# Spare products on TensorE, tiny scalings on ScalarE and a new listed order in a block-sparse attention and channel-mix kernel

## Chip, cores and metric

One core of a Trainium2 chip runs the whole program. The metric is the device time of one execution in microseconds (us). The kernel before takes 536.89 us, the median of three runs (535.77 to 537.21).

## What is computed

The input is four batches of eight heads, 768 positions of 64 features. A position belongs to one of 24 blocks of 32. The first and the last block attend to everything and are seen by all; every other block sees itself, its two neighbours, the two end blocks and three sampled ones. What attention gives is the input x of a channel mix.

```python
scores = np.where(mask, scale * q @ k.T, -1e9)
attn = np.exp(scores - max); attn = attn / (attn.sum(-1) + 1e-09)
x = attn @ v                                     # heads side by side: (4, 768, 512)
xk = mu_k * x + (1.0 - mu_k) * x_prev            # x_prev: x one position earlier
xr = mu_r * x + (1.0 - mu_r) * x_prev
k = np.maximum(xk @ w_k, 0.0)                    # 512 -> 1024
v = k * k @ w_v                                  # 1024 -> 512
return 1.0 / (1.0 + np.exp(-(xr @ w_r))) * v
```

The weights arrive as 64-bit floats.

## The kernel before

The batches are handled in two pairs. **Attention** of a pair is twelve units: one for the two end blocks (the wide unit, m = -1 in the names), eleven for two inner blocks each. In a unit, TensorE multiplies queries and keys (`s`, for the wide unit `sw`), VectorE masks and takes maxima (`nm`), ScalarE takes exponentials with the sums (`p`, `L`), TensorE turns the result over (`t`, copied to `pt`) and multiplies it with the values (`o`). `finish` (line 594) adds 1e-09 to the sums, takes reciprocals (both in `recip`, on VectorE, tile `R`), divides (`x`), and TensorE turns `x` over (`tx`), from where ScalarE copies it to `xt`. The first three units of the first pair (`direct`) add their mask on TensorE; `first_soft` (line 496) then takes four maxima in one reduction (`most`, L500) and scales the 128x4 result by -1/8 (L502), both on VectorE.

The **channel mix** works on tiles of 128 positions of a pair. `split_x` (line 682) takes the difference of neighbouring positions (`d`, L702, on VectorE or GpSimd), adds mu times it to x (`f`, L705), and cuts the result into a high and a low part. `gate` (`r`), `hidden` (`h`) and `products` (`v`) then multiply three terms of high and low parts on TensorE; this is most of its work. `weight` (line 258) prepares each of ten pieces of 1 MB of the weights: ScalarE brings the upper words into range (`wf`, L270), VectorE shifts and puts bits together (L275, L279, L282) or GpSimd multiplies by a sign (L287), then the high part (`w`, L180 or L182) and the low part (`w`, L289) are written. All ten are needed before the first `v` bank is complete.

What runs where, and when, is not decided in this code: every step is added to a plan, the strings in `PICK` name an engine for each step of a kind, and `ORDER` lists all steps. Each engine gets its steps in that order and works them off one after another, waiting on each for what it needs. Transfers are issued by the Sync engine (SP) in the same list.

```python
def spin(times, first=False, last=False):
    one = nc.const_aps.tensor(1.0, (P, 512), BF16)
    for i in range(times):
        nc.tensor.matmul(idle.ap, one[:, 0:P], one, ...)
plan.add(PE, lambda: spin(WARM, first=True), writes=[(idle,)])      # WARM = 10
plan.add(PE, lambda: spin(1, last=True), writes=[(idle,)])
```

These products of ones give nothing that is used. Ten stand at the start and one later.

Of the kernel before, what the change touches and what calls it, by code (L numbers as in the profile page):

```python
# [159 lines left out]
def block_sparse_attention_channel_mix(ctx: ExitStack, tc: tile.TileContext, kt, kd, kw, qw, qn, vt, vn, vw, blocks, own_near, mu_k, mu_r, w_k, w_v, w_r, out):  # L160
# [280 lines left out]
    turns_done = [0]  # L441
# [55 lines left out]
    def first_soft(s, p, nm, L, gi):  # L497
# [548 lines left out]
```

## Time and profile before

| what | value |
|---|---|
| median of 3 runs | 536.89 us (535.77 to 537.21) |
| the profiled execution | 534.2 us, span 532.4 us |
| TensorE matmul busy | 506.9 us, 95% of the span |
| VectorE busy | 370.9 us, 70% |
| ScalarE busy | 295.1 us, 55% |
| GpSimd busy | 238.4 us, 45% |
| mean granted TensorE clock | 0.99 |
| data read from HBM | 80.07 MB |

The span is the time from the first to the last instruction of one execution; 1.8 us of that execution lie around it. Busy shares are averages over the span: in the slices of the page TensorE shows 5 to 8 tenths in the first seven of forty and 9 in all later ones but the last.

### The profile page before, as it was taken

The page shows a single profiled execution, that of the slowest core. Times are in us where ns is not written, and L with a number is a line of the kernel's source. Part 1 is how long each engine was busy: PE and PEld are TensorE (multiplying, and loading weights), DVE is VectorE, ACT ScalarE, POOL GpSimd, SP SyncE. Part 2 cuts the span into 40 slices and gives each one's busy share as a digit, 9 for nine tenths or more (in the row PEclk, how much of TensorE's full clock was granted, in tenths as well). Part 3 has the DMA queues.
Part 4 walks back from the last instruction along what each step waited for, and adds up shares of the span by engine and source line. Part 5 has one row for each costly group of instructions (what it writes and reads, how often), then busy time and mean ns, then how long its engine had stood idle before and what let it go on. Part 6 is the DMA issues. An engine that isn't in the chain of part 4 may idle for free.

```text
span 532.4 us, 17563 instructions
## 1 busy us (share of the span) xinstructions
PE 506.9 (95%) x6911; PEld 407.6 (77%) x6911; DVE 370.9 (70%) x890; ACT 295.1 (55%) x728; POOL 238.4 (45%) x289
## 2 busy tenths in 40 slices
PE   7885799999999999999999999999999999999997
PEld 2554578878878878787887887888888878888886
DVE  5778899997686676579686787776787464635312
ACT  3778698975764672664365567464664353313212
POOL 0571356731851811255073265262367536726530
PEclk9997899999999999999999999999999999999999
DMA  8989786533777887658667877777856603000102
GB/s 295 402 300 324 242 313 216 199 127 115 221 224 230 239 278 231 210 179 271 202 197 265 269 214 219 234 213 228 271 161 183 200 25 95 0 21 20 41 1 79
DMA packets 48165, 103.23 MB, mean 194 GB/s; under 512 B 6929, under 2 KB 23442, under 8 KB 48082
## 3 DMA queue, kind: packets, MB, share of 16 engines
q1 hardware_dynamic: 47794, 101.72, 59.8%
q8 instruction: 54, 0.88, 0.7%
q10 hardware_dynamic: 288, 0.39, 0.2%
q14 instruction: 29, 0.24, 0.1%
HBM read 80.07 MB, written 6.29 MB: 162 GB/s over the span
## 4 chain that ended last, share of the span: by engine, by line
PE 56%; DVE 9%; SPq 6%; DMA 6%; issue 5%; ACT 2%; POOL 2%; DVEq 0%; ACTq 0%; POOLq 0%
PE v L777 18%; PE o L554 5%; PE r_0p L731 4%; DMA VR<-vt 3%; PE s L524 3%; PE r_1p L731 3%; SPq L471 3%; PE h_0p L751 3%; PE h_1p L751 3%; PE h_3p L751 2%; DVE p L435 2%; SPq L414 2%; PE h_2p L751 2%; DMA p<-tb 2%; DMA VR<-vw 1%
## 5 line engine op out<-in xcount | busy, mean ns | idle before, releaser
L777 PE MATMUL v<-w,k 128*128 128x512 f32 (+1 forms) x600 | 143.1, 389 | 0.3 <-DVE w L289 0.3
L777 PEld LDWEIGHTS v<-w,k 128*128 128x128 f32 x600 | 107.5, 188 | 25.6 <-issue 1.6
L435 DVE CUSTOM_DVE_ANT_1 p<-s,near_mask 128x256 f32<-128x256 f32 x152 | 84.9, 627 | 31.0 <-PE s L524 20.4
L440 ACT ACTIVATE p<-p,nm 128x256 f32<-128x256 f32 x152 | 76.3, 503 | 36.4 <-DVE nm L435 31.3
L467 DVE STREAM_TRANSPOSE tb<-p 128x1024 f32<-128x1024 f32 x30 | 37.0, 1236 | 14.7 <-ACT p L440 8.7
L524 PE MATMUL s<-KR,q 64*32 64x256 f32 x1216 | 38.6, 380 | 1.2 <-ACT KR L180 1.2
L780 DVE SCALAR_TENSOR_TENSOR z<-v,z 128x512 f32<-128x512 f32 (+1 forms) x25 | 16.5, 665 | 30.5 <-PE v L777 23.7
L554 PEld LDWEIGHTS o<-VR,p 128*32 128x32 f32 x1920 | 27.9, 110 | 7.7 <-issue 4.9
L180 ACT COPY KR<-keys 128x256 f32 (+1 forms) x71 | 25.6, 426 | 13.6 <-PE s L524 13.4
L554 PE MATMUL o<-VR,p 128*32 128x64 f32 x1920 | 30.4, 220 | 2.7 <-DMA VR<-vt 2.7
L182 POOL COPY KR<-keys 128x256 f32 (+2 forms) x52 | 21.7, 460 | 21.5 <-DMA v_ring<-vw 13.9
L731 PE MATMUL r_1p<-w,xr 128*128 128x512 f32 x120 | 30.7, 401 | 0.0
L524 PEld LDWEIGHTS s<-KR,q 64*32 64x32 f32 x1216 | 20.8, 106 | 12.5 <-issue 3.6
L731 PE MATMUL r_0p<-w,xr 128*128 128x512 f32 x120 | 30.3, 400 | 0.0
L440 ACT ACTIVATION_READ_ACCUMULATOR p<-p,nm 128x1 f32 x152 | 28.7, 189 | 0.0
L741 POOL TENSOR_TENSOR h_1k<-h_1k 128x512 f32<-128x512 f32 x10 | 11.2, 1122 | 34.7 <-ACT k L740 34.7
L731 PEld LDWEIGHTS r_0p<-w,xr 128*128 128x128 f32 x120 | 22.0, 188 | 5.6 <-ACT k L740 0.6
L731 PEld LDWEIGHTS r_1p<-w,xr 128*128 128x128 f32 x120 | 21.9, 188 | 5.3 <-ACT h_3k L739 0.4
L705 DVE SCALAR_TENSOR_TENSOR xr_1f<-xr_1d,mk,xt 128x128 f32<-128x128 f32 x48 | 22.3, 485 | 4.9 <-POOL xr_1d L702 2.9
L751 PE MATMUL h_2p<-xk,w 128*128 128x256 f32 x192 | 25.7, 285 | 0.0
L710 POOL TENSOR_TENSOR xr<-xr_0f,xr 128x256 fp32r<-128x256 f32 x11 | 8.3, 751 | 38.8 <-DVE xr L182 25.1
L751 PE MATMUL h_3p<-xk,w 128*128 128x256 f32 x192 | 24.9, 283 | 0.0
(209 smaller groups left out, 1103.2 us busy)
## 6 DMA issues: line engine op xcount, KB each, us to landing
VR<-vn SPq DMA_DIRECT2D x42, 512.0 KB, 4.7
VR<-vt SPq DMA_DIRECT2D x130, 128.0 KB, 3.5
p<-tb SPq DMA_DIRECT2D x120, 128.0 KB, 3.3
KR<-kd SPq DMA_DIRECT2D x18, 512.0 KB, 4.9
out<-z SPq DMA_DIRECT2D x23, 256.0 KB, 3.6
q<-qn SPq DMA_DIRECT2D x22, 256.0 KB, 4.8
keys<-kw SPq DMA_DIRECT2D x14, 384.0 KB, 6.4
raw<-w_k SPq DMA_DIRECT2D x4, 1024.0 KB, 7.5
```

The costliest lines, as they stand in the source:

```text
L180: nc.scalar.copy(to, of)
L182: engine(on).tensor_copy(to, of)
L435: nc.vector.tensor_tensor_reduce(out=dealt(p.ap[:, cs]), in0=cut(view()), in1=by, scale=-SCALE, scalar=3e+38 if first is None else nm.ap[: ...
L440: plan.add(ACT, lambda: nc.scalar.activation(p.ap[:, cs], p.ap[:, cs], AF.Exp, bias=nm.ap[:, col:col + 1], scale=-1.0, accum_out=L.ap[:, h ...
L467: plan.add(DVE, lambda: nc.vector.transpose(out=turned.ap.rearrange('p (k y c) -> p k y c', k=QB, c=BLK), in_=p.ap.rearrange('p (y k c) -> ...
L524: nc.tensor.matmul(s.ap[ROWS[j], row, a * 256:(a + 1) * 256].rearrange('p (x g a) -> p g a x' if carried else 'p (x a g) -> p g a x', g=2, ...
L554: nc.tensor.matmul(o.ap[ROWS[j], h * D:(h + 1) * D], held[gi][1](i, g, j), VR[values[j % PAIR][g]].ap[:, j // PAIR, h * D:(h + 1) * D], st ...
L705: nc.vector.scalar_tensor_tensor(out=part(f.ap[:, i, :]), in0=part(d.ap), scalar=mk.ap[:, which, c:c + 1], in1=x.ap[:, two, c, 0:TT], op0= ...
L731: nc.tensor.matmul(pr.ap[:, 0:512], xr.ap[:, a, c, :], wr[c].ap[:, w, :], start=c == 0 and m == 0, stop=c == CC - 1 and m == 2)
L751: nc.tensor.matmul(ph.ap[:, ff * PAIR * TT:(ff + 1) * PAIR * TT], wk[f // 4 * CC + c].ap[:, w, f % 4 * P:(f % 4 + 1) * P], xk.ap[:, a, c, ...
L777: nc.tensor.matmul(pv.ap[:, 0:width], hid[f][2](a), wv[f].ap[:, w, cs], start=f == 0 and m == 0, stop=f == FC - 1 and m == 2)
L780: plan.add(DVE, lambda pv=pv, cs=cs: nc.vector.scalar_tensor_tensor(out=z.ap[:, cs], in0=pv.ap[:, 0:width], scalar=unit, in1=z.ap[:, cs], ...
```

## The change

Three sorts of edit and a new table.

- Eight groups of three spare products (`FILLS, FILL`) may stand anywhere in the order between the first ten and the last one. They write the same unused tile.
- The scaling of the four maxima in the direct units and the addition of 1e-09 to the sums become steps with an engine of their own, VectorE or ScalarE by two new strings in `PICK`; the reciprocal is now a step apart, on VectorE. Five of the six scalings and ten of the 24 additions are given to ScalarE.
- The difference in `split_x` may be replaced, where `PICK` says `A`, by mu times x on ScalarE; the mix then adds (1 - mu) times the earlier position, for which a tile `rest` is made once. Of 72 such choices, of two instructions each, 21 are `A`; GpSimd has 29 in place of 44 and VectorE 22 in place of 28.
- `PICK` and `ORDER` are replaced as a whole.

```diff
+        plan.add(DVE, lambda: nc.vector.tensor_scalar(out=rest.ap, in0=mk.ap, scalar1=-1.0, scalar2=1.0, op0=ALU.mult, op1=ALU.add), reads=[(mk, 0, 1)], writes=[(rest,)])
...
     plan.add(PE, lambda: spin(WARM, first=True), writes=[(idle,)])
+    for i in range(FILLS):
+        plan.add(PE, lambda: spin(FILL), writes=[(idle,)])
     plan.add(PE, lambda: spin(1, last=True), writes=[(idle,)])
...
-        plan.add(DVE, lambda: nc.vector.tensor_scalar(out=nm.ap, in0=nm.ap, scalar1=-SCALE, scalar2=None, op0=ALU.mult), reads=[(nm, 'max')], writes=[(nm, 'max')])
+        def scaled(k=most_done[0] - 1):
+            if chosen('most', k) == ACT:
+                nc.scalar.mul(nm.ap, nm.ap, -SCALE)
+            else:
+                nc.vector.tensor_scalar(out=nm.ap, in0=nm.ap, scalar1=-SCALE, scalar2=None, op0=ALU.mult)
+        plan.pick('most', most_done[0] - 1, scaled, reads=[(nm, 'max')], writes=[(nm, 'max')])
...
-        def recip():
-            nc.vector.tensor_scalar(out=R.ap, in0=L.ap, scalar1=1e-09, scalar2=None, op0=ALU.add)
-            nc.vector.reciprocal(R.ap, R.ap)
+        def summed(k=sums_done[0] - 1):
+            if chosen('sum', k) == ACT:
+                nc.scalar.activation(R.ap, L.ap, AF.Copy, bias=1e-09)
+            else:
+                nc.vector.tensor_scalar(out=R.ap, in0=L.ap, scalar1=1e-09, scalar2=None, op0=ALU.add)
...
                 def dif(c=c, d=d, k=k):
+                    if chosen('dif', k) == ACT:
+                        nc.scalar.activation(part(d.ap), x.ap[:, two, c, 1:1 + TT], AF.Copy, scale=mk.ap[:, which, c:c + 1])
+                        return
...
+FILLS, FILL = (8, 3)
...
-    "near": "PPAA",
+    "sum": "DDDDAADDDDADADDAADAAADDA",
+    "near": "PPPP",
+    "most": "AAADAA",
-    "hi": "PDDAPPAAAD",
-    "lo": "PPDDPDDDDD",
+    "hi": "DDDAAAAAAD",
+    "lo": "DDDPDDDDDD",
...
-    13, 5, 6, 8, 0, 2, 3, 14, 16, 11, 15, 36, 12, 35, 1, 37, 56, 19, 21, 20, 22, 24, 23, 25, 55, 39, 40, 41, 26, 42,
+    2, 13, 0, 119, 3, 15, 14, 24, 20, 22, 28, 27, 23, 45, 44, 21, 64, 65, 84, 25, 31, 85, 112, 16, 29, 114, 30, 33,
```

Three places show what the order becomes.

VectorE from the sums of unit 1 to its division, before. `R_1` are the sums of unit 1, `nm_2_0` and `nm_2_1` the maxima of unit 2, `pt` copies for unit 1, `w_864` a low part of a weight, `x_0` and `x_1` the divisions of units 0 and 1:

```order
L603 TENSOR_SCALAR R_1_859<-L_1_648 128x8
L604 RECIPROCAL R_1_859<-R_1_859 128x8
L613 TENSOR_TENSOR x_0_862<-o_0_766,R_0_579 128x512
L500 TENSOR_REDUCE nm_2_0_887<-s_2_0_866 128x4
L502 TENSOR_SCALAR nm_2_0_887<-nm_2_0_887 128x4
L182 COPY pt_1_1_1_940<-t_1_1_1_930 128x512
L182 COPY pt_1_1_0_948<-t_1_1_0_935 128x512
L500 TENSOR_REDUCE nm_2_1_950<-s_2_1_895 128x4
L182 COPY pt_1_0_0_958<-t_1_0_0_953 128x512
L502 TENSOR_SCALAR nm_2_1_950<-nm_2_1_950 128x4
L289 TENSOR_TENSOR w_864<-wf_650,w_864 128x2x512
L613 TENSOR_TENSOR x_1_1033<-o_1_964,R_1_859 128x512
```

The same stretch on VectorE in the change:

```order
L618 TENSOR_SCALAR R_1_848<-L_1_671 128x8
L504 TENSOR_REDUCE nm_2_0_861<-s_2_0_824 128x4
L182 COPY pt_1_1_0_864<-t_1_1_0_856 128x512
L182 COPY pt_1_1_1_901<-t_1_1_1_843 128x512
L628 TENSOR_TENSOR x_0_922<-o_0_772,R_0_548 128x512
L624 RECIPROCAL R_1_848<-R_1_848 128x8
L504 TENSOR_REDUCE nm_2_1_931<-s_2_1_903 128x4
L247 TENSOR_SCALAR rest<-mk 128x8
L293 TENSOR_TENSOR w_938<-wf_815,w_938 128x2x512
L628 TENSOR_TENSOR x_1_1024<-o_1_943,R_1_848 128x512
```

Both scalings of maxima are gone from VectorE, one `pt` copy went to ScalarE, `rest` came in, and the low part ahead of `x_1` is of another weight.

TensorE behind the wide unit's turned result (`tx_-1`) and ahead of the first products with values (`o_0`), before:

```order
L608 MATMUL tx_-1_685<-ident,x_-1_679 128x128 x4
L449 MATMUL t_0_1_0_705<-ident,p_0_1_562 128x128 x4
L449 MATMUL t_0_0_1_719<-ident,p_0_0_400 128x128 x4
L449 MATMUL t_0_1_1_748<-ident,p_0_1_562 128x128 x4
L449 MATMUL t_1_0_1_756<-ident,p_1_0_647 128x128 x4
```

The same place in the change:

```order
L622 MATMUL tx_-1_699<-ident,x_-1_667 128x128 x4
L253 LDWEIGHTS const-bfloat16-1.0
L253 MATMUL idle<-const-bfloat16-1.0 128x512
...
L453 MATMUL t_0_1_0_736<-ident,p_0_1_473 128x128 x4
L453 MATMUL t_0_0_1_757<-ident,p_0_0_519 128x128 x4
L453 MATMUL t_1_0_1_767<-ident,p_1_0_670 128x128 x4
```

Six spare products (two groups, each product with its weight load) now stand between `tx_-1` and the next turning. The other six groups stand in pairs after the first half of the wide scores (`sw_0`), between `o_1` and `tx_1`, and right behind `tx_1`.

VectorE behind the division of unit 1, before:

```order
L613 TENSOR_TENSOR x_1_1033<-o_1_964,R_1_859 128x512
L275 TENSOR_SCALAR wf_889<-wf_889 128x1024
L282 SCALAR_TENSOR_TENSOR wf_889<-raw_743,wf_889 128x1024
L702 TENSOR_TENSOR xr_0_0d_1087<-xt_0_571 128x128
L705 SCALAR_TENSOR_TENSOR xr_0_0f_1089<-xr_0_0d_1087,mk,xt_0_571 128x128
L702 TENSOR_TENSOR xr_0_0d_1121<-xt_0_571 128x128
L705 SCALAR_TENSOR_TENSOR xr_0_0f_1089<-xr_0_0d_1121,mk,xt_0_571 128x128
```

The same stretch in the change:

```order
L628 TENSOR_TENSOR x_1_1024<-o_1_943,R_1_848 128x512
L279 TENSOR_SCALAR wf_853<-wf_853 128x1024
L286 SCALAR_TENSOR_TENSOR wf_853<-raw_725,wf_853 128x1024
...
L182 COPY KR<-keys_108 128x256
...
L182 COPY KR<-keys_108 128x256
L182 ISA
L182 COPY KR<-keys_108 128x256
L724 SCALAR_TENSOR_TENSOR xr_0_0f_1085<-xt_0_86,rest,xr_0_0d_1054 128x128
L724 SCALAR_TENSOR_TENSOR xr_0_0f_1085<-xt_0_86,rest,xr_0_0d_1087 128x128
```

Three copies of sampled keys came to VectorE here, and the first two differences left it for ScalarE.

## Rows read from the trace of the kernel before

**Rows 1.** Busy time by stretch: start:end, length, then each engine's busy us (instructions), clock, DMA.

```profile
0.00:40.64 40.64, 32.53 (x455) 17.97 (x455) 29.05 (x75) 24.92 (x53) 18.45 (x29) 1.00 0.92 331
40.64:63.87 23.23, 16.24 (x360) 12.10 (x360) 20.30 (x24) 17.70 (x44) 5.79 (x3) 0.78 0.89 301
63.87:110.69 46.82, 43.16 (x751) 34.77 (x751) 46.05 (x91) 42.88 (x110) 25.74 (x21) 1.00 0.62 216
...
111.00:480.00 369.00, 365.66 (x5112) 301.92 (x5112) 258.18 (x673) 196.20 (x500) 168.23 (x215) 1.00 0.63 192
```

**Rows 2.** Timeline of TensorE at the two cuts: start, duration, instruction, wait before it.

```profile
38.41 1.61 PE L592 MATMUL o_-1_249<-v_ring,ptw 128*64 128x64 f32 x46 [0.73 <-DMA v_ring<-vw]
...
110.73 1.43 PE L777 MATMUL v<-w,k 128*128 128x512 f32 x5 [0.32 <-DVE w L289]
```

**Rows 3.** TensorE's waits from 106 us on: total us, times, longest.

```profile
PE o L554 <- DMA VR<-vt: 2.7, 4, 1.2
```

**Rows 4.** Timeline of all engines, 40 to 112 us: small VectorE operations, GpSimd beside them, `x_1`.

```profile
41.24 0.15 DVE L502 TENSOR_SCALAR nm<-nm 128x4 f32<-128x4 f32 x1
...
52.82 2.04 DVE L603 TENSOR_SCALAR R<-L 128x8 f32<-128x8 f32 x1 [1.35 <-ACT p L507]
...
56.02 2.35 POOL L289 TENSOR_TENSOR w<-wf,w 128x1024 fp32r<-128x1024 f32 x1
...
56.82 1.57 DVE L502 TENSOR_SCALAR nm<-nm 128x4 f32<-128x4 f32 x1
...
63.87 0.69 DVE L613 TENSOR_TENSOR x<-o,R 128x512 f32<-128x512 f32 x1 [1.22 <-PE o L554]
```

**Rows 5.** VectorE's groups of instructions, 40.64 to 63.87 us: count, busy us, mean ns, idle.

```profile
L275 DVE TENSOR_SCALAR wf<-wf 128x1024 int32<-128x1024 int32 x3 | 2.0, 683 | 0.0
...
L182 DVE COPY pt<-t 128x512 f32<-128x512 f32 x3 | 2.0, 682 | 0.0
```

**Rows 6.** VectorE's groups, 63.87 to 110.69 us; the key copies from the groups of 0 to 111 us.

```profile
L182 DVE CAST xk<-xk_0f 128x512 fp32r<-128x512 f32 x2 | 1.2, 616 | 0.1
...
L702 DVE TENSOR_TENSOR xr_0d<-xt 128x128 f32<-128x128 f32 x2 | 0.6, 284 | 0.0
...
L182 DVE CAST xr<-xr_0f 128x256 fp32r<-128x256 f32 x1 | 0.3, 295 | 0.0
...
L182 DVE COPY KR<-keys 128x256 f32 x3 | 1.1, 395 | 1.1 <-DMA raw<-w_r 1.1
```

**Rows 7.** Timeline of VectorE, 40 to 112 us: the sums of unit 3.

```profile
88.50 1.26 DVE L603 TENSOR_SCALAR R<-L 128x8 f32<-128x8 f32 x1
```

**Rows 8.** Chain of waits up to 112 us: start, us, two masked maxima back to back.

```profile
83.45 1.01 DVE p L435 x2
```

**Rows 9.** Timeline of TensorE, 30 to 112 us, around the places of the spare products.

```profile
35.81 0.59 PE L479 MATMUL s<-first_mask,ident 128*128 128x512 bf16 x2 [0.66 <-ACT p L507]
...
49.40 3.42 PE L554 MATMUL o<-VR,pt 128*32 128x64 f32 x118 [1.81 <-DMA VR<-vn]
...
60.65 3.15 PE L554 MATMUL o<-early,pt 128*32 128x64 f32 x128
64.71 0.63 PE L608 MATMUL tx<-ident,x 128*128 128x128 f32 x4 [0.92 <-DVE x L613]
...
66.95 1.10 PE L524 MATMUL s<-KR,q 64*32 64x256 f32 x32 [1.17 <-ACT KR L180]
```

**Rows 10.** The page's costliest groups: count, busy us, mean ns of one, idle before.

```profile
L777 PE MATMUL v<-w,k 128*128 128x512 f32 (+1 forms) x600 | 143.1, 389 | 0.3 <-DVE w L289 0.3
```

**Rows 11.** Chain of waits of the whole span: value products of a later unit.

```profile
258.42 1.92 PE o L554 x128
```

**Rows 12.** Busy time by stretch (columns as in the first group), short stretches with a low clock.

```profile
46.00:48.00 2.00, 1.59 (x16) 1.02 (x14) 1.97 (x3) 0.00 (x0) 0.00 (x0) 0.51 1.02 387
...
60.00:62.00 2.00, 2.00 (x56) 1.67 (x58) 1.96 (x4) 2.00 (x6) 0.00 (x0) 0.50 1.00 362
```

**Rows 13.** ScalarE's groups of the whole span: the smallest plain conversion.

```profile
L180 ACT CAST xr<-xr_0f 128x256 fp32r<-128x256 f32 x9 | 3.6, 404 | 12.9 <-DVE xr_0f L705 12.9
```

More of the change, by code (lines that the diff above doesn't have):

```diff
@@ L199, in block_sparse_attention_channel_mix @@
     mk = fixed([P, 2, CC], F32, 'mk')
+    rest = fixed([P, 2, CC], F32, 'rest')
     early = [buf([P, 2, PAIR, DM], F32, f'w{5 * CC // 2 - 1 - i}', 1, f'early{i}') for i in range(EARLY_V // 2)]
@@ L440, in exp @@
         plan.add(ACT, lambda: nc.scalar.activation(p.ap[:, cs], p.ap[:, cs], AF.Exp, bias=nm.ap[:, col:col + 1], scale=-1.0, accum_out=L.ap[:, h:h + 1]), reads=[(p, *keys), (nm, col)], writes=[(p, *keys), (L, h)])
-    turns_done = [0]
+    turns_done, most_done, sums_done = ([0], [0], [0])
     def turn(parts, name):
@@ L501, in first_soft @@
         plan.add(DVE, most, reads=[(s,)], writes=[(nm, 'max')])
-        plan.add(DVE, lambda: nc.vector.tensor_scalar(out=nm.ap, in0=nm.ap, scalar1=-SCALE, scalar2=None, op0=ALU.mult), reads=[(nm, 'max')], writes=[(nm, 'max')])
+        most_done[0] += 1
+        def scaled(k=most_done[0] - 1):
[4 more added lines that the diff above has]
+        plan.pick('most', most_done[0] - 1, scaled, reads=[(nm, 'max')], writes=[(nm, 'max')])
         for i in range(4):
@@ L600, in finish @@
             tp = buf([P, CC, P], F32, 't', T_BUFS, f'tx{b}_{m}', ps)
[L602 to L604 removed]
+        sums_done[0] += 1
+        def summed(k=sums_done[0] - 1):
[3 more added lines that the diff above has]
+                nc.vector.tensor_scalar(out=R.ap, in0=L.ap, scalar1=1e-09, scalar2=None, op0=ALU.add)
         def tr():
@@ L608, in tr @@
                 nc.tensor.transpose(tp.ap[:, c, :], x.ap[:, c * P:(c + 1) * P], ident.ap)
-        plan.add(DVE, recip, reads=[(L, *range(H))], writes=[(R,)])
+        plan.pick('sum', sums_done[0] - 1, summed, reads=[(L, *range(H))], writes=[(R,)])
+        plan.add(DVE, lambda: nc.vector.reciprocal(R.ap, R.ap), reads=[(R,)], writes=[(R,)])
         def divide():
@@ L701, in dif, with mix @@
                 def dif(c=c, d=d, k=k):
+                    if chosen('dif', k) == ACT:
+                        nc.scalar.activation(part(d.ap), x.ap[:, two, c, 1:1 + TT], AF.Copy, scale=mk.ap[:, which, c:c + 1])
+                        return
                     engine(chosen('dif', k)).tensor_tensor(out=part(d.ap), in0=x.ap[:, two, c, 1:1 + TT], in1=x.ap[:, two, c, 0:TT], op=ALU.subtract)
-                def mix(d=d, c=c, i=i, f=f):
+                def mix(d=d, c=c, i=i, f=f, k=k):
+                    if chosen('dif', k) == ACT:
+                        nc.vector.scalar_tensor_tensor(out=part(f.ap[:, i, :]), in0=x.ap[:, two, c, 0:TT], scalar=rest.ap[:, which, c:c + 1], in1=part(d.ap), op0=ALU.mult, op1=ALU.add)
+                        return
                     nc.vector.scalar_tensor_tensor(out=part(f.ap[:, i, :]), in0=part(d.ap), scalar=mk.ap[:, which, c:c + 1], in1=x.ap[:, two, c, 0:TT], op0=ALU.mult, op1=ALU.add)
-                plan.pick('dif', k, dif, reads=[(x, *known)], writes=[(d,)])
-                plan.add(DVE, mix, reads=[(d,), (x, *known), (mk, which)], writes=[(f, i)])
+                plan.pick('dif', k, dif, reads=[(x, *known), (mk, which)], writes=[(d,)])
+                plan.add(DVE, mix, reads=[(d,), (x, *known), (mk, which), (rest,)], writes=[(f, i)])
             cs = slice(h * MIX, (h + 1) * MIX)
@@ L881 @@
 PICK = {
-    "turn": "DADAAAADADAAAAAADADDAAAAAAAADAAAAAADADAAAADADDDDDDDD",
-    "near": "PPAA",
-    "keys": "AAPDAPAPAAAAAAAADAPAPAADAAPPPPPDDAAPDAPAPADAAPAA",
+    "turn": "AAAADDAAAAADAAAAAADDAAAAAADDAAAAAADADDAAAAADDAADDDDA",
+    "sum": "DDDDAADDDDADADDAADAAADDA",
+    "near": "PPPP",
+    "keys": "AAPPPDPADAPAAAAADADDADADAAPAAPDDAPAPAPPPPPAAAAAA",
+    "most": "AAADAA",
     "mag": "AAAAAAAAAA",
     "sign": "PPDDPDPPDD",
-    "hi": "PDDAPPAAAD",
-    "lo": "PPDDPDDDDD",
-    "dif": "DPPPPPDPPPPDPPDPPDPPDDPDDPDDPDDPDPPDPDPDDPPPPDPDPPPPPDPPPDPDPPDPPDDDPDPP",
-    "mix": "DADDAAADADDDDDDAADDAADDADDAAADDDADDDDADADDDDDADDADDDDDDDDDADADDADDADDDDA",
-    "low": "DDDDDDPDDPPDDPPPDPDDDPPDDDDPDPPPDPDPPPPDDDDPPDPPDDDPPDDPPPDPPDPPDDDDDDPD",
+    "hi": "DDDAAAAAAD",
+    "lo": "DDDPDDDDDD",
+    "dif": "APPPPADAAPPDAPDDPDPAPPDPPADPDAPADPPDAPPAPPDPAPADDADADPDPDDDAAAPPPDADADAP",
+    "mix": "DAADADADADDDDADDDDDADDADDADDDADDDDDDDAAADDDDADDDDADDADAADADDAAADADAADDAD",
+    "low": "DDDDDDPDDPPDPPDDDDPDDDPPPPPDDPPPDDPPDPPPPDPPPPDDDPDDPDPDPPDDPPDDDDDPDDDP",
 }
 ORDER = [
[103 rows of a table removed]
[105 rows of a table added]
 ]
```

206 rows, old and new, of the table ORDER are left out of this document.

## The prediction

> **What bounds the kernel now.** I began with the busy time by stretch, cutting the run where VectorE divides the wide unit (40.64 us), where it divides unit 1 (63.87), and where it writes the last low part of a weight (110.69) [rows 1]. In the order PE, weight loads, VectorE, ScalarE, GpSimd the reader should see this: from 111 to 480 us TensorE is busy 365.66 of 369 us, so nothing but TensorE counts there; from 63.87 to 110.69 VectorE is busy 46.05 of 46.82, so VectorE sets when that stretch ends; from 40.64 to 63.87 VectorE has 20.30 of 23.23 and the DMA engines 0.89; before 40.64 the DMA engines have 0.92 and no engine is full. Next the timeline of TensorE at the cuts: the first ends when the last piece of the ring of values has landed (`o_-1`, 0.73 us of waiting for DMA), the last when the last low part is there (`v` waits 0.32 for VectorE) [rows 2]. Last the waits of TensorE behind 106 us: the largest is four waits for values, 2.7 us together [rows 3]. So a change is worth what it does to the moment of that last low part, plus any wait that it opens in the packed stretch. TensorE's useful work behind that moment is the same in both kernels.
>
> **Up to 40.64 us: 0.** VectorE takes on a conversion of a weight, one shift (both about 0.68, as L275 [rows 5]) and two low parts (at most 2.35 each, what GpSimd needs for one [rows 4]): under 6.1 us. It idles 40.64 - 29.05 = 11.6 us here [rows 1], and that cover goes only if all this lands behind the last value piece, which comes by the same transfers as before.
>
> **40.64 to 63.87 us: -3.1.** The scalings of maxima leave VectorE. By itself one takes 0.15 us; one that begins while GpSimd is in a 2.35 us product takes 1.57, and an addition to sums, as small, 2.04 [rows 4]. Three scalings stood here: -1.57 - 0.15 - 0.15. One `pt` copy goes to ScalarE (-0.68) and one shift went ahead of 40.64 (-0.68) [rows 5]. `rest` comes in, 128x8 like the sums; I take it clean, +0.15. Sum -3.1. The low end is -4.3: then the 1.22 us that `x_1` waits for `o_1` goes too [rows 4]. The high end is -1.2: `rest` stalls as the sums did, 2.04. I take the clean value because GpSimd has one low part left in this stretch and lost three conversions; the scalings on ScalarE go where it has 23.23 - 17.70 = 5.5 us idle [rows 1]. Late next, once VectorE is quicker, is `o_1`.
>
> That stall is where a rule of the Trainium skill speaks against the change: "Advanced Engine Details and Errata", section "VectorE Performance Modes", says that VectorE's second SBUF port is shared with GpSimd, and that the two block each other. The trace agrees (1.57 beside GpSimd, 0.15 without). By that rule any small addition left on VectorE can still stall, whoever took the scalings; its time is in the second rival.
>
> **63.87 to 110.69 us: +0.6.** VectorE is full here, so each operation counts. In: three copies of keys, +1.1; one conversion of `xr`, +0.3; one more `pt` copy, +0.7; two masked maxima, +1.0 [rows 5, 6, 8]. Out: one conversion of `xk`, -0.6; two differences, -0.6 [rows 6]; the addition to the sums of unit 3, -1.26 [rows 7]. Sum +0.6. Low end -0.4, if the two maxima merely took the place of other work; high end +1.9, if the 1.26 stall passes to another small operation. The two differences cost ScalarE at most 0.40 each, its smallest conversion of twice as many elements [rows 13]; it idles 3.9 us here.
>
> **Spare products: +0.5.** Two products of this shape take 0.59 us [rows 9], and one of 512 columns lasts 0.389 by itself [rows 10], so each further one adds about 0.20 and a pair of groups, six products, takes between 1.2 (in line) and 1.4 (by itself); I take 1.3. The pair behind `sw_0` lies beside waits of 0.66 and 0.73 [rows 2, 9]. The pair behind `tx_-1` lies ahead of `o_0`, which waits 1.81 for values anyway [rows 9]. The pair before `tx_1` lies in its 0.92 us of waiting for the division: +0.4; the pair behind it in the 1.17 that the next scores wait for keys: +0.1 [rows 9]. At half clock each product takes 0.4 and the two pairs cost +2.7; below nothing they can only go through the clock.
>
> **Clock: -0.6.** The granted clock is 0.51 around 47 us and 0.50 around 61 us, the 1.2 GHz level, each time behind stretches in which TensorE waited [rows 12]. `o_0` takes 3.42 and `o_1` 3.15 there [rows 9], the same products 1.92 at full clock [rows 11]. `o_1` is on VectorE's path, since `x_1` waits for it. At full clock -1.2, unchanged 0; I take half, because the spare products stand at some of the waits ahead of it.
>
> **Behind 111 us: 0.** ScalarE takes on 42 scalings of `x` and 15 tiny ones, under 0.40 each [rows 13]: 23 us at most, against 369 - 196 = 173 idle in the packed stretch alone [rows 1]. GpSimd loses work. Best case -2.7, all four waits for values gone [rows 3]; worst case in the third rival.
>
> **Sum:** -3.1 - 0.6 + 0.6 + 0.5 = -2.6 us. The profiled execution took 534.2 and would take 531.6; the median, 2.7 above it, goes from 536.89 to **534.3 us**. With the ends of single terms this case lies between 531 and 536.
>
> **Rivals.**
> 1. *The spare products hold the clock.* Then `o_0` takes 1.92 (-1.5) and `o_1` gains 1.2 where I took 0.6: 534.3 - 1.5 - 0.6 = 532.2 us. For it: two of the pairs lie in the very gaps behind which the clock was low. Against it: two pairs stand behind `o_1`, too late for it, and `o_0` waits 1.81 for its values, so a faster `o_0` needs an earlier transfer only in part. The Trainium skill, "TensorE: Matmul & The Clock Gate", section "HAM oscillation — how this bites in real kernels", says that a wait between bursts of matmuls drops the clock, so that the next burst starts cold. The trace agrees with the drop (0.51 behind the waits); that spare work prevents it, no run here shows.
> 2. *No change.* Up to 64 us the DMA engines are 0.92 and 0.89 busy [rows 1]. The same bytes pass, in another order; if `o_0` and the weights go on waiting for them, VectorE's saving becomes idle time: 536.9. Or the stalls stay: `rest` at 2.04 and the two left-over additions give -2.6 + 1.9 = -0.7, so 536.2. For it: `o_-1` and `o_0` stand waiting for transfers [rows 2, 9]. Against it: from 63.87 on VectorE is back to back without any wait for DMA. That the change doesn't do what it says is in here: the listed place of an instruction is not its time.
> 3. *Slower: values late in the packed stretch.* The place is TensorE's `o` behind 110 us, which waits four times for values, 0.7 each on average [rows 3]. A new order can put these products ahead of their transfers, and TensorE, working its list in order, then stands with all `r`, `h` and `v` queued behind. Priced by the wait of `o_0`, 1.81 [rows 9], four cost 7.2 instead of 2.7: +4.5 - 2.6 = +1.9, so 538.8 us. It decides once such waits grow by more than 2.6 us. For it: this stretch has 3.3 us of slack in 369, so no wait is hidden there. Against it: the DMA engines are at 0.63 there and have room [rows 1].
>
> **How the numbers follow.** About 0.3% (1.6 us) can be told from no change: below 535.3 is faster, above 538.5 slower. The forecast has 0.50 (0.42 faster, 0.08 same), since VectorE's rows carry it and the packed stretch leaves the work alone. The clock rival has 0.12, all faster. No change has 0.20 (0.02, 0.16, 0.02); slower has 0.18 (0.01 same). Together 0.56 faster, 0.25 same, 0.19 slower. The low end of the range is the lower ends of the three VectorE and clock terms, -4.3 - 1.2 - 0.4, with the 1.5 of the first rival: -7.4, 529.5 us. The high end is all high ends with no wait in the packed stretch, -1.2 + 1.9 + 2.7 = +3.4, or about 540.5, which holds the third rival too.
>
> **What the profile after should show.** The last low part of a weight near 108 us instead of 110.7; VectorE busy about 17 us between its divisions of the wide unit and unit 1, where it was 20.3; no scaling or sum of over 1 us in the stretch; scalings on ScalarE of some 0.2 to 0.4 us; `o_1` at 2 to 3 us; in the packed stretch a TensorE share of 0.99 and waits for values of about 2.7 us in all. I am wrong in the first term if `rest` or a sum takes 2 us or `x_1` comes no earlier than 63 us; wrong about the packed stretch if TensorE's idle time there grows by over 2 us; wrong about the clock if `o_0` shrinks to 2 us, or if the low clock spreads beyond 64 us.

## The result and the profile after

The changed kernel takes 528.52 us, the median of 20 runs (525.91 to 533.64); the kernel before took 533.65 in the 20 runs beside it. The ratio is 0.9915, with a 95% interval from 0.9888 to 0.9942. The same kernel run again among the experiments (e5) gave 528.76 against 532.48, ratio 0.9946 (0.9922 to 0.9969). The ratios here and below come from the single executions, without those over 1.5% above the fastest of their kernel, and are not the quotients of the medians beside them, which would be 0.9904 and 0.9930. So the change takes off 0.5 to 0.9%, 2.9 to 4.5 us (3.7 to 5.1 by the medians). The forecast was a gain of 2.6 us, 0.48%; its time, 534.3, and the low end of its range, 529.5, both lie too high.

The page after: the busy share of TensorE, its weight loads, VectorE, ScalarE and GpSimd, and the chain of work that ended last, by engine.

```profile
PE 510.8 (97%) x6935; PEld 407.3 (77%) x6935; DVE 355.7 (67%) x866; ACT 313.2 (59%) x785; POOL 213.5 (41%) x257
...
PE 77%; DMA 7%; SPq 5%; DVE 4%; ACT 4%; issue 2%; ACTq 0%; DVEq 0%
```

The chain of the page before:

```profile
PE 56%; DVE 9%; SPq 6%; DMA 6%; issue 5%; ACT 2%; POOL 2%; DVEq 0%; ACTq 0%; POOLq 0%
```

The busy time by stretch, cut at the same events as [rows 1]: division of the wide unit, division of unit 1, end of the last low part of a weight. Columns as there.

```profile
0.00:40.42 40.42, 34.27 (x461) 18.05 (x462) 29.72 (x75) 25.28 (x55) 14.62 (x30) 0.96 0.94 339
40.42:58.28 17.86, 14.27 (x367) 9.60 (x368) 15.48 (x20) 16.47 (x42) 5.73 (x3) 1.00 0.83 291
58.28:104.22 45.94, 45.16 (x757) 35.63 (x756) 43.51 (x96) 41.87 (x109) 22.72 (x21) 1.00 0.72 253
111.00:480.00 369.00, 366.58 (x5051) 302.28 (x5050) 248.16 (x640) 210.30 (x542) 153.65 (x187) 1.00 0.63 192
```

Against [rows 1] the three stretches are 0.2, 5.4 and 0.9 us shorter. TensorE is now busy 45.16 of the 45.94 us of the third stretch, where it had 43.16 of 46.82; VectorE fell from 46.05 to 43.51. So in this profile the bound has moved: TensorE is busy for 98% of the third stretch, and in the chain VectorE has 4% where it had 9%. The clock of the second stretch is 1.00 where it was 0.78. Behind 106 us TensorE's waits for values, 2.7 us in [rows 3], are now 1.1:

```profile
PE o L565 <- DMA VR<-vn: 0.8, 1, 0.8
...
PE o L565 <- DMA VR<-vt: 0.3, 1, 0.3
```

VectorE and GpSimd between 48 and 60 us (timeline: start, duration, instruction, wait before it), which answers to [rows 4]:

```profile
49.17 1.23 DVE L286 SCALAR_TENSOR_TENSOR wf<-raw,wf 128x1024 int32<-128x1024 int32 x1
50.32 0.16 DVE L618 TENSOR_SCALAR R<-L 128x8 f32<-128x8 f32 x1
...
50.53 2.42 POOL L291 TENSOR_TENSOR wf<-wf,raw 128x1024 f32<-128x1024 f32 x1 [10.39 <-DMA early<-vn]
...
52.90 2.38 POOL L293 TENSOR_TENSOR w<-wf,w 128x1024 fp32r<-128x1024 f32 x1
53.47 0.68 DVE L628 TENSOR_TENSOR x<-o,R 128x512 f32<-128x512 f32 x1
54.06 0.19 DVE L624 RECIPROCAL R<-R 128x8 f32<-128x8 f32 x1
...
56.08 0.21 DVE L247 TENSOR_SCALAR rest<-mk 128x8 f32<-128x8 f32 x1
...
58.28 0.69 DVE L628 TENSOR_TENSOR x<-o,R 128x512 f32<-128x512 f32 x1 [0.86 <-PE o L565]
```

The addition to the sums of unit 1 now begins 0.21 us ahead of a GpSimd product and takes 0.16 us, where it began inside one and took 2.04. The product of before in which it began:

```profile
52.43 2.40 POOL L287 TENSOR_TENSOR wf<-wf,raw 128x1024 f32<-128x1024 f32 x1 [11.84 <-ACT raw L286]
```

`rest` takes 0.21. No scaling is left on VectorE here.

TensorE, timeline, which answers to [rows 2, 9]:

```profile
45.72 1.17 PE L565 MATMUL o<-VR,pt 128*32 128x64 f32 x64
...
52.18 1.09 PE L565 MATMUL o<-VR,pt 128*32 128x64 f32 x60 [1.71 <-issue]
...
56.56 1.66 PE L565 MATMUL o<-early,pt 128*32 128x64 f32 x104 [0.23 <-issue]
58.15 1.48 PE L253 MATMUL idle<-const-bfloat16-1.0 128*128 128x512 bf16 x6
...
104.79 1.64 PE L798 MATMUL v<-w,k 128*128 128x512 f32 x6
```

`o_0` and `o_1` run at full clock, and the products with the last piece of the weights (the 19th `v` product and on) begin at 104.79 without a wait, 0.57 us after its low part was done. Before, the 19th began at 109.94 and the 20th, at 110.73, after the wait in [rows 2]:

```profile
109.94 0.48 PE L777 MATMUL v<-w,k 128*128 128x512 f32 x1
```

The scalings and additions on VectorE, by the groups of the whole span (count, busy us, mean ns), of the kernel before and then of the change; the additions of the wide units, two before and one after, stand apart at 0.2 us each:

```profile
L603 DVE TENSOR_SCALAR R<-L 128x8 f32<-128x8 f32 x22 | 10.6, 484 | 2.5 <-ACT p L507 1.4 <-ACT p L440 1.2
L502 DVE TENSOR_SCALAR nm<-nm 128x4 f32<-128x4 f32 x6 | 4.7, 777 | 0.1
```

```profile
L618 DVE TENSOR_SCALAR R<-L 128x8 f32<-128x8 f32 x13 | 2.8, 217 | 1.6 <-ACT p L444 1.6
L512 DVE TENSOR_SCALAR nm<-nm 128x4 f32<-128x4 f32 x1 | 0.2, 239 | 0.0
```

These 28 tiny operations took 15.3 us; the 14 that are left take 3.0.

### The profile page after: what moved, and what is told of

Read it like the earlier page. It is cut to its first block, busy times and chain, and to the rows that moved or that the text cites. A ratio compares the mean times of both kernels' runs of the same rounds, so it can differ in the third digit from the quotient of the medians.

```text
span 527.1 us, 17633 instructions
## 1 busy us (share of the span) xinstructions
PE 510.8 (97%) x6935; PEld 407.3 (77%) x6935; DVE 355.7 (67%) x866; ACT 313.2 (59%) x785; POOL 213.5 (41%) x257
## 4 chain that ended last, share of the span: by engine, by line
PE 77%; DMA 7%; SPq 5%; DVE 4%; ACT 4%; issue 2%; ACTq 0%; DVEq 0%
PE v L798 21%; PE o L565 7%; PE s L535 5%; PE r_0p L752 5%; PE r_1p L752 5%; PE h_3p L772 4%; PE h_2p L772 4%; PE h_1p L772 3%; PE h_0p L772 3%; DMA VR<-vn 2%; SPq L418 2%; DMA VR<-vt 2%; SPq L475 2%; PE sw L581 2%; DMA p<-tb 2%
## 5 line engine op out<-in xcount | busy, mean ns | idle before, releaser
L798 PE MATMUL v<-w,k 128*128 128x512 f32 (+1 forms) x600 | 141.5, 388 | 0.1
L182 POOL COPY KR<-keys 128x256 f32 (+2 forms) x54 | 22.9, 462 | 27.8 <-DMA keys<-kw 13.7
L731 POOL TENSOR_TENSOR xr<-xr_1f,xr 128x256 fp32r<-128x256 f32 x10 | 7.4, 739 | 53.0 <-ACT xr L180 39.9
L762 POOL TENSOR_TENSOR h_0k<-h_0k 128x512 f32<-128x512 f32 x10 | 10.6, 1063 | 38.7 <-ACT k L761 38.7
L772 PE MATMUL h_0p<-xk,w 128*128 128x256 f32 x192 | 25.0, 284 | 0.0
L772 PEld LDWEIGHTS h_1p<-xk,w 128*128 128x128 f32 x192 | 23.5, 189 | 1.6 <-ACT h_0k L760 0.8
```

What stands on the lines that cost most here:

```text
L182: engine(on).tensor_copy(to, of)
L762: plan.add(POOL, lambda: nc.gpsimd.tensor_tensor(out=kk.ap, in0=kk.ap, in1=kk.ap, op=ALU.mult), reads=[(kk,)], writes=[(kk,)])
L772: nc.tensor.matmul(ph.ap[:, ff * PAIR * TT:(ff + 1) * PAIR * TT], wk[f // 4 * CC + c].ap[:, w, f % 4 * P:(f % 4 + 1) * P], xk.ap[:, a, c, ...
L798: nc.tensor.matmul(pv.ap[:, 0:width], hid[f][2](a), wv[f].ap[:, w, cs], start=f == 0 and m == 0, stop=f == FC - 1 and m == 2)
```

## The experiments

Fifteen kernels, each with one profile and 12 timed runs beside runs of the kernel before. Half the interval of a ratio is 0.0022 to 0.0034, so 1.2 to 1.8 us.

### The two kernels again

**e5** is the change, unaltered.

> The changed kernel itself, unaltered, on the chip and in the rounds of its neighbours: what they are compared with. If nothing but noise lies between chips: 0.9915 of the kernel before, within its interval.

528.76 us, ratio 0.9946. Unit 1 is divided at 58.61 us and the 19th `v` product begins at 104.44. But `o_0` was caught by a late transfer, and the clock with it:

```profile
47.88 1.57 PE L565 MATMUL o<-VR,pt 128*32 128x64 f32 x56 [2.15 <-DMA VR<-vn]
...
48.00:52.00 4.00, 4.00 (x91) 2.10 (x89) 2.01 (x4) 3.19 (x6) 1.90 (x1) 0.57 0.89 343
```

Spare products and all, the clock was 0.57 from 48 to 52 us, and this execution, with a span of 525.6 us, was still 1.5 us shorter than that of the first profile. So a low clock at `o_0` need not make an execution long.

**e9** is the kernel before, unaltered.

> The kernel before, unaltered: a second profile of it. Theory of stalls: the scalings and the sums of unit 1 last about as long as they overlap a GpSimd product (1 to 2 us each where they begin inside one), and unit 1 is divided between 60 and 64 us. Rival, that the profile before was an unlucky one: unit 1 at 61 us or earlier and the last low part near 107 us, without a stall over 1 us between 40 and 64 us.

533.59 us, ratio 0.9992 (0.9963 to 1.0021). Of its profiled execution, with a span of 538.8 us, the stalls:

```profile
53.24 2.41 POOL L287 TENSOR_TENSOR wf<-wf,raw 128x1024 f32<-128x1024 f32 x1 [11.75 <-DMA early<-vn]
53.63 2.05 DVE L603 TENSOR_SCALAR R<-L 128x8 f32<-128x8 f32 x1 [1.25 <-ACT p L507]
...
56.83 2.34 POOL L289 TENSOR_TENSOR w<-wf,w 128x1024 fp32r<-128x1024 f32 x1
57.64 1.56 DVE L502 TENSOR_SCALAR nm<-nm 128x4 f32<-128x4 f32 x1
...
65.45 0.69 DVE L613 TENSOR_TENSOR x<-o,R 128x512 f32<-128x512 f32 x1 [1.71 <-PE o L554]
```

The stalls come again, 2.05 and 1.56 where [rows 4] have 2.04 and 1.57: the profile before was no accident. Both end with the GpSimd product in which they began: 53.63 + 2.05 = 55.68 against 53.24 + 2.41 = 55.65, and 59.20 against 59.17. The same holds throughout: over the 17 profiles 84 additions, scalings or makings of `rest` on VectorE begin inside a GpSimd instruction, at least 0.2 us ahead of its end, and 83 of them end within 0.05 us of that end.

### Spare products, tiny steps and order: all eight combinations

With the two kernels themselves, six more cover every combination of the spare products, of the scalings and additions on ScalarE, and of the new order (with all else in the table and the differences on ScalarE).

**e1**, the change without spare products (ORDER loses their eight steps):

```diff
-FILLS, FILL = (8, 3)
+FILLS, FILL = (0, 3)
```

> The changed kernel without its eight groups of spare products; order and engines of everything else as in the change. Clock theory (the spare products hold TensorE at full clock, and that gives most of the time beyond the forecast): the granted clock between the divisions of the wide unit and unit 1 falls from 1.00 to about 0.8, the products o_0 and o_1 take 3 us each in place of about 2.2, and the last low part of a weight comes some 2 to 3 us after its 104.2 us; about 531 us against the change's 528.5. Order theory (the listed order and VectorE's relief give all of it, spare products only fill waits): clock stays at 1.00 or its fall costs nothing, time 528 to 529, perhaps 1 us less since 2.9 us of spare products around tx_1 are gone.

529.96 us, ratio 0.9947 (0.9923 to 0.9972): level with e5 (0.9946). **e4**, the change with the tiny steps on VectorE:

```diff
-    "sum": "DDDDAADDDDADADDAADAAADDA",
+    "sum": "DDDDDDDDDDDDDDDDDDDDDDDD",
...
-    "most": "AAADAA",
+    "most": "DDDDDD",
```

> The changed kernel with all scalings of maxima and all additions to the sums back on VectorE. If the forecast's first term was right (stalls of 1.3 to 2 us leave VectorE with them): scalings at 1 us or more reappear between 40 and 60 us, the division of unit 1 comes 1 to 2 us later, time about 530. If TensorE and its clock set the startup: VectorE has waits of 0.7 to 0.9 us for TensorE there which take up most of it, time within 0.7 us of 528.5.

531.19 us, ratio 0.9988 (0.9964 to 1.0013). One stall of over a microsecond came back, again up to the end of a GpSimd product (54.32 against 54.28):

```profile
51.86 2.42 POOL L291 TENSOR_TENSOR wf<-wf,raw 128x1024 f32<-128x1024 f32 x1 [10.61 <-DVE R L618]
52.97 1.35 DVE L512 TENSOR_SCALAR nm<-nm 128x4 f32<-128x4 f32 x1
```

Over the whole span the 28 tiny operations took 8.2 us here (7.7 in e6, without spare products), so the new order nearly halves the 15.3 of before, and ScalarE takes off another 5. From the division of the wide unit to that of unit 1 it is 17.6 us here (41.61 to 59.24), no longer than in the change; what comes later is the division of the wide unit. **e6**, both edits at once:

> The changed kernel without spare products and with all scalings and additions back on VectorE; left of the change are its order, its engines for copies and parts of weights, and the differences on ScalarE. If each of the two edits is worth what the two runs without one of them hint at (1.7 us for the spare products, 3.8 for the scalings) and they add up, the change loses all its gain: about 533, the same as before or slower. If both only prepare the same moment, the last low part of a weight, one of them suffices and this one comes out at about 531.

531.59 us, ratio 0.9996 (0.9966 to 1.0027): order, table and differences alone give nothing that can be measured. The stretch of stalls is short all the same, 18.0 us (42.50 to 60.45). **e3**, the kernel before with the eight groups at the same places of its own order (the single spare product that came later stands behind them):

```diff
+    for i in range(FILLS):
+        plan.add(PE, lambda: spin(FILL), writes=[(idle,)])
...
+FILLS, FILL = (8, 3)
```

> The kernel before with the same eight groups at the same places of its own order (behind sw_0, behind tx_-1, between o_1 and tx_1, behind tx_1), nothing else changed. Clock theory: the clock from 40.64 to 63.87 us rises from 0.78 to 0.9 or more, o_0 or o_1 falls towards 1.9 us, and the time drops by 1 to 2.5 us to about 531.5. Order theory: no more than 0.5 us either way, since VectorE ends the stretch and o_0 waits for a transfer.

531.20 us, ratio 0.9988 (0.9958 to 1.0017), with a mean granted clock of 1.00 in the profiled execution. VectorE and GpSimd there, between 51 and 59 us:

```profile
51.62 0.16 DVE L605 TENSOR_SCALAR R<-L 128x8 f32<-128x8 f32 x1
...
51.83 2.42 POOL L289 TENSOR_TENSOR wf<-wf,raw 128x1024 f32<-128x1024 f32 x1 [11.02 <-DMA early<-vn]
...
53.74 0.54 DVE L504 TENSOR_SCALAR nm<-nm 128x4 f32<-128x4 f32 x1
...
55.44 2.39 POOL L291 TENSOR_TENSOR w<-wf,w 128x1024 fp32r<-128x1024 f32 x1
...
57.12 0.74 DVE L504 TENSOR_SCALAR nm<-nm 128x4 f32<-128x4 f32 x1
...
58.90 0.68 DVE L615 TENSOR_TENSOR x<-o,R 128x512 f32<-128x512 f32 x1
```

Nothing was done to these steps, and yet the three operations shrank from 3.8 us (2.04 + 1.57 + 0.16) to 1.4, because they fell at other moments of the same GpSimd products: the addition just ahead of one, the scalings nearer to an end (54.28 against 54.25, 57.86 against 57.83). The stall is not a fixed price of an operation; it lasts from its begin to the end of the product. **e7**, the kernel before with five scalings and ten additions on ScalarE:

```diff
+            if chosen('most', k) == ACT:
+                nc.scalar.mul(nm.ap, nm.ap, -SCALE)
...
+            if chosen('sum', k) == ACT:
+                nc.scalar.activation(R.ap, L.ap, AF.Copy, bias=1e-09)
...
+    "most": "AAADAA",
+    "sum": "DDDDAADDDDADADDAADAAADDA",
```

> The kernel before with the same five scalings and ten additions on ScalarE, each addition right behind the last exponential of its unit in the list; order otherwise untouched, no spare products. Forecast's first term: three scalings and the stalled addition leave VectorE between 40 and 64 us, so unit 1 is divided 1.5 to 2.5 us earlier, about 1.5 to 2.5 us faster than before. If the scalings pay only in the order that was searched with them, or ScalarE's queue delays them as much: within 0.7 us of before.

529.22 us, ratio 0.9959 (0.9933 to 0.9984): a gain on the old order. Unit 1 is divided 20.5 us behind the wide unit (39.82 to 60.35), where it was 23.2: 2.7 less, where the forecast gave 1.9 to the three scalings. What it leaves is the sums of unit 1, which stay on VectorE in this string and stall as before:

```profile
51.85 2.41 POOL L287 TENSOR_TENSOR wf<-wf,raw 128x1024 f32<-128x1024 f32 x1 [12.44 <-ACT raw L286]
52.24 2.04 DVE L615 TENSOR_SCALAR R<-L 128x8 f32<-128x8 f32 x1 [1.44 <-ACT p L514]
```

**e8**, the edits of e3 and e7 together:

> The kernel before with the eight groups of spare products and the scalings and additions on ScalarE, its own order. With this the eight kernels cover every combination of spare products, scalings and order. If the two edits carry the gain: 528.5 to 529.5, as the change. If the new order carries most of it: 531 to 532.

530.23 us, ratio 0.9966 (0.9938 to 0.9994): between its two theories, and no better than e7.

| ratio to before (clock, median of the runs) | neither | spare products | tiny steps on ScalarE | both |
|---|---|---|---|---|
| order before | 1 (0.990) | 0.9988 (0.996) | 0.9959 (0.993) | 0.9966 (0.997) |
| order of the change | 0.9996 (0.987) | 0.9988 (0.997) | 0.9947 (0.990) | 0.9915 and 0.9946 (0.997) |

Each edit is read from the four pairs that differ in it alone; for the change the mean of its two ratios, 0.9930, is taken. The tiny steps: -0.0058, -0.0049, -0.0041, -0.0022, on average -0.0043 or 2.3 us. The spare products: -0.0017, -0.0008, -0.0012, +0.0007, on average -0.0007 or 0.4 us. The order with the rest: -0.0036, -0.0012, 0, -0.0004, on average -0.0013 or 0.7 us. Four pairs of such ratios carry about 0.002 either way, so only the first of the three is shown. The clock tells the spare products apart in every pair (0.990 to 0.996, 0.993 to 0.997, 0.987 to 0.997, 0.990 to 0.997), the time in none.

### How many spare products, and where

**e2** keeps the first four groups, **e14** the last four, **e13** has two and **e12** six products in each group.

e2 and e14 (ORDER loses the steps that are left out):

```diff
-FILLS, FILL = (8, 3)
+FILLS, FILL = (4, 3)
```

e13, and e12 with a 6 in the same place:

```diff
-FILLS, FILL = (8, 3)
+FILLS, FILL = (8, 2)
```

> The changed kernel with only its first four groups (behind sw_0 and behind tx_-1); the four around tx_1 are left out. Clock theory: o_0 runs at full clock as in the change (the groups behind tx_-1 stand ahead of it); o_1 too, since the later groups come only behind it; time 527 to 528.5, as 2.9 us of spare products are gone from a TensorE that has no wait there, unless the clock falls behind 58 us, which would cost up to 2 us. Order theory: the same as the run without any groups, 528 to 529.

530.35 us, ratio 0.9954 (0.9929 to 0.9979), clock 0.994.

> The changed kernel with only the four groups around tx_1; those behind sw_0 and tx_-1 are left out. If the clock is lost ahead of o_0 only: clock 0.990 to 0.992 as without any group, and time 1 us above the run without any, 530 to 531, since these groups lie on TensorE's path behind unit 1. If these groups are what pays: clock 0.995 or more and 528.5 to 529.

529.81 us, ratio 0.9945 (0.9912 to 0.9979), clock 0.990.

> The changed kernel with two products in each of its eight groups. If the first products buy the clock and the others only cost their 0.18 us each: clock 0.996 to 0.997 still, time 1 us less than the change, 527.5 to 528. If the clock follows the number of products: clock near 0.994, time 529 to 529.5.

530.62 us, ratio 0.9936 (0.9905 to 0.9968), clock 0.997.

> The changed kernel with six products in each of its eight groups, 24 more in all, about 0.24 us each: 2.9 us more behind sw_0 and tx_-1, 2.9 us more around tx_1. If the groups around tx_1 lie on the path: from the division of unit 1 to the last products of the first tile 2 to 2.9 us more, time 531 to 532. If they lie in waits: less than 0.7 us more. If they buy clock: full clock from 40 to 64 us, and o_0 at full clock even where its values come late.

532.49 us, ratio 1.0021 (0.9990 to 1.0053), clock 0.998. From none to three products a group, in all places or some, the ratios from 0.9954 to 0.9915 can't be told apart. The last four groups by themselves win no clock (0.990, as without any), the first four about half of it. Six products cost some 4 us more than three did in e5 (5.6 by the change's first ratio), for 24 products more. In its profile twelve of them show on the path, in the two groups around `tx_1`:

```profile
56.84 2.80 PE L253 MATMUL idle<-const-bfloat16-1.0 128*128 128x512 bf16 x12
...
59.92 2.78 PE L253 MATMUL idle<-const-bfloat16-1.0 128*128 128x512 bf16 x12
```

Each pair of groups takes 2.8 us where it took 1.48. From the division of unit 1 (56.98) to the 19th `v` product (104.96) it is 48.0 us, against 46.5 and 45.8 in the two profiles of the change. That is 1.5 to 2.2 of the 4 us; where the rest goes was not found.

### Three edits beside these

**e10** turns the 21 letters A of `dif` into P (differences on GpSimd):

```diff
-    "dif": "APPPPADAAPPDAPDDPDPAPPDPPADPDAPADPPDAPPAPPDPAPADDADADPDPDDDAAAPPPDADADAP",
+    "dif": "PPPPPPDPPPPDPPDDPDPPPPDPPPDPDPPPDPPDPPPPPPDPPPPDDPDPDPDPDDDPPPPPPDPDPDPP",
```

**e11** starts with sixteen spare products:

```diff
-WARM = 10
+WARM = 16
```

**e15** has every scaling and addition on ScalarE:

```diff
-    "sum": "DDDDAADDDDADADDAADAAADDA",
+    "sum": "AAAAAAAAAAAAAAAAAAAAAAAA",
...
-    "most": "AAADAA",
+    "most": "AAAAAA",
```

> The changed kernel with its 21 choices of a scaling of x on ScalarE turned into differences on GpSimd. Forecast: ScalarE's scalings lie beside other work, so no change beyond 0.8 us, 528 to 530; the division of unit 1 is untouched. Rival: they relieve GpSimd in the packed stretch; then the waits of TensorE there grow by over 1 us and the time is 530 or more.

529.96 us, ratio 0.9954 (0.9932 to 0.9976): within noise of the change.

> The changed kernel with sixteen in place of ten spare products at the start. Clock theory: the first wide scores run at full clock, the wide unit is divided up to 1 us earlier unless its values hold it, and the time is 0 to 1 us less. Transfer theory: the wide unit's division stays between 39.5 and 40.5 us, no change.

530.00 us, ratio 0.9951 (0.9928 to 0.9974). The wide unit is divided at 39.20 us against 40.42 and 40.03, and the 19th `v` product comes at 104.43: nothing gained.

> The changed kernel with all six scalings and all 24 additions on ScalarE. If VectorE's thirteen remaining additions (2.8 us, 0.217 each) still stall something on the path: 0.5 to 1 us less, about 528. If they lie beside waits, or ScalarE's queue is late with them: no change within 0.7 us, or 1 us more where a reciprocal now waits for ScalarE.

531.04 us, ratio 0.9955 (0.9919 to 0.9990): no gain left in the other additions. No kernel tried is faster than the change beyond its interval.

### From the startup to the end

The start of the 19th `v` product is the end of the startup. What TensorE does behind it is the same work in every kernel. Before, it began at 109.94 and 422.5 us followed to the end of the span; in e6, e7 and e8 it began at 106.25 to 107.96 and 421.8 to 422.6 followed; in e9 it began at 111.55 and 427.3 followed. In the twelve profiles where it began before 106 us, the change and e5 among them, 421.2 to 426.3 followed, on average 424.0. With one profile of each kernel and this scatter it is not shown that a shorter startup gives part of its gain away again: the five others average 423.2 with e9 and 422.2 without. TensorE's waits for values there vary from 0.2 to 5.2 us from profile to profile and do not explain the rest by themselves. What makes it vary by 5 to 6 us stays open.

## Why the prediction was right or wrong

Three steps failed: the base, which lay 3.2 us high; the first VectorE term, which left the stall of the sums where it was; and the third stretch, which had the wrong sign. The direction, and the tiny steps as the main cause, came out as forecast.

**The base.** The time was counted from 536.89, the median of three runs. The 20 runs beside the change gave 533.65, and 134 more beside the experiments have a median of 532.7: those three runs, which are among the 20, lay 3 to 4 us high. From 533.65 the same sum gives 531.05, and the range would have held 528.52. The absolute time failed at this step, which took the three runs as they stood. (The terms of the high end, +3.4, give 540.3 from 536.89, not 540.5.)

**Up to 40.64 us: 0.** The number was right for the two profiles of the change, 40.42 and 40.03 (e5), with 29.72 us of VectorE's work in the first where there were 29.05. But the transfers alone did not set the 40.64, as the forecast has it. It overlooked a fourth scaling, which stalls until the end of a GpSimd product (39.59 against 39.56) and holds up the reduction right ahead of the wide unit's division; that division then begins without a wait:

```profile
37.21 2.35 POOL L289 TENSOR_TENSOR w<-wf,w 128x1024 fp32r<-128x1024 f32 x1 [0.81 <-DVE R L603]
...
38.57 1.02 DVE L502 TENSOR_SCALAR nm<-nm 128x4 f32<-128x4 f32 x1
...
40.64 0.68 DVE L613 TENSOR_TENSOR x_-1_679<-o_-1_249,R_-1_495 128x512 f32<-128x512 f32 x1
```

In e7, with that scaling on ScalarE, it waits for `o_-1` and comes earlier:

```profile
39.82 0.69 DVE L625 TENSOR_TENSOR x_-1_679<-o_-1_249,R_-1_495 128x512 f32<-128x512 f32 x1 [1.33 <-PE o_-1_249 L599]
```

In the five profiles with the tiny steps on VectorE the wide unit is divided at 40.64 to 42.50 us, on average 41.4, in the twelve others at 38.76 to 40.88, on average 39.7. So some 1.7 of the 2.3 us of the tiny steps show here already, where the forecast had nothing; that they reach the end of the span was not tried by itself.

**40.64 to 63.87 us: -3.1, and -0.6 for the clock.** The size was too small: -5.4, and in e5 -4.7 (18.58 us). The three scalings and the copy went as written. What failed is the step that lets the sums of unit 1 stay as they were. They stayed on VectorE, but the new order puts them 0.2 us ahead of the GpSimd product instead of 0.4 us inside it, and 2.04 us became 0.16. With that -1.9 the first term is -5.0. The addition had waited 1.35 us for ScalarE's exponentials and begun at 52.82 [rows 4]; it now finds them done and begins at 50.32. The forecast priced what left VectorE, not when the rest would begin. `rest` took 0.21, near the 0.15 taken.

This is no accident of one profile. The product begins 0.14 us after VectorE's last bit operation on the piece that it multiplies (L286, up to 50.40), in all twelve profiles of the new order, also in e15, where no addition stands behind that operation. In the eleven others the addition is VectorE's next step, finds its exponentials done, begins 0.21 or 0.22 us ahead of the product and takes 0.16 or 0.17; so it is in e3, in the old order. In the four profiles in which the exponentials are late (before, e7, e8, e9) it waits 1.25 to 1.44 us for them, begins 0.4 us after the product and takes 2.04 or 2.05. The length of the stretch goes with these sums more than with the scalings. In those four it takes 20.5 to 23.9 us, in the thirteen others 17.0 to 20.1, with the scalings back on VectorE in e3, e4 and e6 among them (18.0, 17.6, 18.0). That the scalings shorten this stretch in the new order, as the forecast's mechanism has it, is not shown; in the old one e7 agrees with it.

The rule on the SBUF port of the Trainium skill ("Advanced Engine Details and Errata", "VectorE Performance Modes") is narrower than the forecast gave it: it speaks of VectorE's "2p" instructions, those that use two read ports, and its table marks `tensor_scalar` for them and `tensor_tensor` not. The trace agrees: `TENSOR_SCALAR` begun inside a GpSimd product ends with it, while the division `x_0`, a `TENSOR_TENSOR`, took 0.68 inside the product of 52.90 to 55.28. A `RECIPROCAL` of 128x8, which the table does not list, took 0.19 there, at 54.06. So an addition left on VectorE stalls only where it begins inside a product.

**63.87 to 110.69 us: +0.6, and +0.5 for the spare products.** Wrong in sign: 45.94 us after 46.82, -0.9, and 45.94 in e5. TensorE made little of it: the 20th `v` product, which waited for the last low part before, began 46.86 us behind the division of unit 1 before (63.87 to 110.73), 46.83 after (58.28 to 105.11) and 46.15 in e5. The counts were right, the durations were not constant. Four groups of the weights and their means show it, before and then after:

```profile
L289 DVE TENSOR_TENSOR w<-wf,w 128x1024 fp32r<-128x1024 f32 x5 | 7.2, 1451 | 0.0
L282 DVE SCALAR_TENSOR_TENSOR wf<-raw,wf 128x1024 int32<-128x1024 int32 x5 | 6.8, 1356 | 0.1
L275 DVE TENSOR_SCALAR wf<-wf 128x1024 int32<-128x1024 int32 x5 | 4.1, 820 | 0.0
L279 DVE SCALAR_TENSOR_TENSOR wf<-raw,wf 128x1024 int32<-128x1024 int32 x3 | 3.9, 1302 | 0.1
```

```profile
L286 DVE SCALAR_TENSOR_TENSOR wf<-raw,wf 128x1024 int32<-128x1024 int32 x5 | 6.3, 1269 | 0.1
L293 DVE TENSOR_TENSOR w<-wf,w 128x1024 fp32r<-128x1024 f32 x5 | 6.2, 1247 | 0.1
L283 DVE SCALAR_TENSOR_TENSOR wf<-raw,wf 128x1024 int32<-128x1024 int32 x3 | 3.7, 1223 | 0.0
L279 DVE TENSOR_SCALAR wf<-wf 128x1024 int32<-128x1024 int32 x5 | 3.6, 718 | 1.2 <-ACT wf L274 1.2
```

The same eighteen instructions take 22.0 us before and 19.8 after, 2.2 less, while GpSimd is busy 22.72 us in place of 25.74. That GpSimd's work is what lengthens them is likely by the stalls above, but was not tried by itself.

**Clock and spare products.** The forecast's net of -0.1 for the two is close to the -0.4 of four pairs, which is itself not told apart from nothing. The clock rival was right in the clock: 0.997 instead of 0.990. At 0.990, 2% of the span at half clock, TensorE spends some 10.6 us at half clock, at 0.997 some 3.2. Its time did not follow. e5 is a plain example against the rival: 0.57 for 4 us, and the shortest span of all 17. The Trainium skill's rule on waits between bursts ("TensorE: Matmul & The Clock Gate", "HAM oscillation — how this bites in real kernels") says that the clock drops in a wait, and the trace agrees (0.57 behind 2.15 us of waiting in e5). Whether the next products are on the path, the profile has to tell.

**Behind 111 us: 0.** Waits for values went down from 2.7 to 1.1 us in the first profile, so the slower rival found no ground. In the first pair of profiles the rest of the span is the same, 422.5 and 422.4 us: nearly the whole difference of 5.3 us lies in the startup.

**No change.** This rival fell by the intervals, though the new order by itself (e6) did give no change. What the eight kernels show is 2.3 us for the tiny steps, with about 1 us either way; what the spare products and the order add to it can't be told from nothing.

## What to carry to other kernels

Where a small operation stalls because another engine is in a long one, ask at which moment it will begin, not only which engine runs it: the same addition cost 2.04 us where it began 0.4 us after a GpSimd product did, and 0.16 where it began 0.2 us before it. Look also at what releases the long operation: done right behind that step, the small one came first every time (eleven profiles of the new order and e3), and where it had to wait for another engine it came too late. A clock that is won is worth time only where TensorE's products end the chain; measure the clock and the time apart. And before an absolute time is forecast to half a per cent, see how far single runs of the kernel scatter (here 7.5 us over 20 runs): the median of three missed the base by more than the whole forecast gain.

## What the runs showed of the hardware

- A `TENSOR_SCALAR` on VectorE of 128x4 or 128x8 that begins inside a GpSimd product of 128x1024 ends with that product (2.05, 1.56, 1.35 and 2.04 us instead of 0.16; 83 of 84 begun inside any GpSimd instruction end within 0.05 us of its end). A `RECIPROCAL` of 128x8 in such a place took 0.19, and 147 of 151 do not end with the GpSimd instruction. I had expected the stall to fall on all small operations alike.
- On ScalarE the scaling of 128x4 takes 0.21 us and the addition of 128x8 0.20, the means of five and nine in the profile of the change, though GpSimd works beside them too.
- Behind a wait of 2.15 us for a transfer the clock was 0.57 (e5), although spare products had run until some 3 us ahead of that wait.
